# Row gathers one group ahead, unordered scatters and a ring of five weight buffers in the expert stage of a routed feed-forward kernel

## The chip, the cores and the metric

The kernel runs on one core of a Trainium2 chip. The metric is the device time of one execution in microseconds (us). Five engines of the core matter here: PE (TensorE, the matmuls; PEld is its weight load), DVE (VectorE), ACT (ScalarE), POOL (GpSimd, which issues the indirect transfers, that is gathers and scatters of rows by a list of row numbers) and SP (SyncE, which issues the plain transfers). Each engine works through its own instructions in order, and waits where an instruction needs what another engine or a transfer has not finished.

## What is computed

The reference runs three stages: an attention over packed tokens, a dense feed-forward with SiLU, and a routed one, in which every token goes to the one expert of eight that has its largest logit. Cut to what matters here:

```python
x = attention(q, k, v, p)                 # 4608 tokens x 512
x = silu(x @ w_in) @ w_out                # 512 -> 2048 -> 512
e_idx = argmax(x @ w_gate)                # one expert of 8 for each token
gate_w = softmax(x @ w_gate)[e_idx]
eom = sigmoid(x @ w_output_gate)
for e in range(8):                        # w1[e]: 512 x 1024, w2[e]: 1024 x 512
    mask = e_idx == e
    out[mask] = gate_w[mask] * eom[mask, e] * (relu(x[mask] @ w1[e]) @ w2[e])
```

Every matrix product is made of two or three products of high and low parts of its operands (names that end in `hi` and `lo`), so that float32 accuracy is kept.

## The kernel before

The first two stages run over eight batches of 576 tokens (`batch`, 16 steps `f` each). While they run, the finished rows go to an HBM table `xr` of one row per token (512 values and the routing weight). `place` works out for every token its place in its expert's list, and POOL scatters the token's number to that place in an HBM table of positions. Of that table there are two copies (`NPERM`), written in turn and added up when they are read.

The expert stage (`experts`, `groups`) works on groups of 576 tokens of one expert. Eight groups are always run (`NSTATIC`); more are run under a condition on the number of groups. The largest expert's first group, group 0, is started inside the last batch (`open_first`); the list of the other groups is known only when the last rows have been placed (`table`, `spread`).

One group has eight steps, one for each 128 of the 1024 hidden columns. `up(n)` is 24 matmuls into the accumulator `pu`, of which there is one, so that ACT and DVE must have read it (L992, L993) before the next `up`. `down(n)` is 14 matmuls into five accumulators `py` (blocks j of 128 tokens; block 4 has 64 tokens and is done first). The order on PE is written out by hand: `up(n+1)`, then `down(n)`. Between them lie numbered gaps: gap 2n+1 stands behind `up(n+1)`, gap 2n+2 behind `down(n)`. The dictionary `gaps` says what else is issued in each gap:

- `fetch(g)` gets a group's tokens: SP loads the 576 row numbers from the position tables (`fetch_ix`, L907 and L908) and the expert's output-gate row (`og`, L929), POOL adds the two copies (L910, L911) and gathers five blocks of rows from `xr` into `xg` (`fetch_x`, L920). There is one buffer `xg`. Fetch of group k+1 stands in gap 16k+1, which is one step into group k.
- `trx(g, j)` transposes block j on PE into one PSUM bank `px` (L960), ACT and DVE copy it out as high and low part into `xt` (two buffers, one for each of two groups), and DVE and ACT work out the output gate. For group k+1 the five blocks stand in gaps 16k+5 to 16k+13.
- `load_chunk` has SP load a quarter of an expert's weights, two transfers of 1 MB each (L945, L947), into a ring of seven buffers (`RING`). From step 5 on one is issued behind every odd `down`, into the buffer that this `down` has just finished with.

When the last `down` of a group ends, `put_out` scales the five blocks out of PSUM into `y` (ACT L1023 for j below 4; L1028 to L1030 for block 4), of which there are four buffers, and POOL scatters them to the rows of `out` (L1031). Every scatter writes the whole of `out` as far as the ordering of the program knows, so each waits until the one before it has landed.

Of the kernel before, what the change touches and what calls it, by code (L numbers as in the profile page):

```python
# [21 lines left out]
DM = 512  # L22
# [18 lines left out]
RING = 7  # L41
FG = F2 // 128
NPERM = 2
# [3 lines left out]
def constants():  # L47
# [14 lines left out]
    t -= NTOK // NPERM  # L62
# [27 lines left out]
class Kernel:  # L90
    def __init__(self, tc, ins, out):
        self.tc, self.nc, self.i, self.out = tc, tc.nc, ins, out
        nc = tc.nc
        self.ws1 = nc.dram_tensor("ws1", (E8, 4, 2, 128, F2), F32, kind="Internal").ap()
        self.ws2 = nc.dram_tensor("ws2", (E8, 4, 2, 128, 2 * DM), F32, kind="Internal").ap()
        self.perm = [nc.dram_tensor(f"perm{i}", (PROWS, PW), I32, kind="Internal").ap() for i in range(NPERM)]
        self.xr = nc.dram_tensor("xr", (NTOK + 1, XW), F32, kind="Internal").ap()
# [5 lines left out]
    def run(self):  # L103
# [18 lines left out]
        self.pick_i = cp.tile([128, 8], U32, name="pick_i")  # L122
        self.ptab = cp.tile([1, 2], I32, name="ptab")
# [52 lines left out]
    def setup_late(self):  # L176
# [6 lines left out]
        nc.gpsimd.memset(fill, NTOK // NPERM)  # L183
        for perm in self.perm:
            nc.sync.dma_start(perm.rearrange("(p c) w -> p (c w)", p=128).rearrange("p (h n) -> p h n", h=2),
                              fill.unsqueeze(1).to_broadcast([128, 2, n]))
# [18 lines left out]
    def open_first(self, f):  # L205
# [18 lines left out]
        if f > 12:  # L224
            for j in ((0, 1), (2, 3), (4,))[f - 13]:
                self.trx(0, j)

    def last_rows(self):
# [8 lines left out]
        acc = self.ps_acc.tile([128, 512], F32, tag="acc3", name="accL")  # L237
        side = {2: lambda: self.row_t(g, 3, 0), 4: lambda: self.row_logits(g, 3, 0), 5: lambda: self.row_logits2(g, (3, 0)),
# [547 lines left out]
    def place(self, g):  # L786
# [15 lines left out]
        def put():  # L802
# [48 lines left out]
    def experts(self):  # L851
# [19 lines left out]
    def more(self, lo, hi):  # L871
        self.nload = 4 * lo
        self.fetch(lo)
        for _ in range(RING):
            self.load_chunk()
        for j in range(GB):
            self.trx(lo, j)
        for k in range(lo, hi - 1):
            self.gaps[16 * k + 1] = [lambda k=k: self.fetch(k + 1)]
            for j in range(GB):  # L880
                self.gaps[16 * k + 5 + 2 * j] = [lambda k=k, j=j: self.trx(k + 1, j)]
        self.groups(lo, hi)
# [6 lines left out]
    def groups(self, lo, hi):  # L889
        self.up(FG * lo)  # L890
        self.gap(2 * FG * lo)
        for n in range(FG * lo, FG * hi):
# [4 lines left out]
            if n % 2 and n > 4 and self.nload < 4 * hi:  # L897
# [3 lines left out]
    def fetch_ix(self, g, off):  # L901
        nc = self.nc
        off = nc.values_load(off, engines=[ENG.SP], min_val=0, max_val=END)
        ix = self.rt.tile([128, NPERM, GB], I32, tag="xix_p", bufs=2, name="xix_p")
        at = self.rt.tile([128, GB], I32, tag="xix", bufs=3, name="xix")
        for i, perm in enumerate(self.perm):
            nc.sync.dma_start(ix[:, i, 0:4], perm[bass.ds(off, 512), 0:1].rearrange("(j p) w -> p (j w)", p=128))  # L907
            nc.sync.dma_start(ix[:64, i, 4:5], perm[bass.ds(off + 512, 64), 0:1])  # L908
# [41 lines left out]
    def trx(self, g, j):  # L950
        nc, rt = self.nc, self.rt
        x, og = self.x[g][0][j], self.x[g][1]
        if j == 0:
            self.sc[g] = rt.tile([128, GB, 4], F32, tag="sc", bufs=2, name="sc")
            if g == 1:
                t = self.p2.tile([128, 8 * GN], F32R, name="xt1")
                self.xt[1] = t.rearrange("p (h k t) -> p h k t", h=2, k=4)
        ps = self.bank("px")
        for k in range(4):
            nc.tensor.transpose(ps[:, 0, k * 128:k * 128 + 128], x[:, k * 128:k * 128 + 128], self.ident)  # L960
        n = min(128, GN - j * 128)
        src = ps[:, 0, :].rearrange("p (k t) -> p k t", k=4)[:, :, :n]
        hi, lo = [self.xt[g % 2][:, i, :, j * 128:j * 128 + n] for i in range(2)]
        nc.scalar.copy(out=hi, in_=src)
        nc.vector.tensor_tensor(out=lo, in0=src, in1=hi.bitcast(F32), op=ALU.subtract)
        junk = rt.tile([128, 512], BF16, tag="junk", bufs=1, name="junk")
# [3 lines left out]
        nc.scalar.activation(out=sc[:, 1:2], in_=sc[:, 0:1], func=AF.Exp, scale=-1.0)  # L970
        nc.vector.tensor_scalar(out=sc[:, 1:2], in0=sc[:, 1:2], scalar1=1.0, scalar2=None, op0=ALU.add)
        nc.vector.reciprocal(out=sc[:, 2:3], in_=sc[:, 1:2])
        nc.vector.tensor_tensor(out=sc[:, 3:4], in0=sc[:, 2:3], in1=x[:, DM:DM + 1], op=ALU.mult)
# [44 lines left out]
    def put_out(self, g, j):  # L1018
        nc, p2, acc = self.nc, self.p2, self.acc[j]
        at, s = self.at[g], self.sc[g][:, j, 3:4]  # L1020
        y = p2.tile([128, DM], F32, tag="y", bufs=4, name="y")
        if j < 4:
            nc.scalar.activation(out=y, in_=acc, func=AF.Copy, scale=s)  # L1023
# [45 lines left out]
```

## Time and profile before

| | us |
|---|---|
| median of 3 runs | 1380.42 (1375.12 to 1380.48) |
| the profiled execution, its own time | 1382.79 |
| its span, first to last instruction | 1381.0 |
| batches and last rows, before the first `up` | 828.48 |
| expert stage on PE, first `up` to last `down` | 529.6 (828.48 to 1358.09) |
| from there to the end of the span | 22.9 |

The profile describes one execution. Its own time is 1.8 us over its span; sums are made against that execution and then put against the median, which is 2.4 us lower. PE is busy for 90% of the span. [...]

### The profile page before, as it was taken

To read this page: it belongs to the slowest core of one execution; us is meant where nothing else is said; L and a number is where in the kernel's file an instruction comes from. 1 tells how busy PE (TensorE), PEld (TensorE's weight loads), DVE (VectorE), ACT (ScalarE), POOL (GpSimd) and SP (SyncE) were. 2 spreads that over 40 slices of the span, in tenths; PEclk is the share of its full clock that TensorE was granted. 3 is DMA by queue.
4 is the path that set the end of the run, shared out by engine and by line. 5 is a ranking of instruction groups with operands and counts; after the bars stand their busy time and mean duration, and the time that the engine had idled before them with its cause. 6 is when DMAs were issued, how large, how long until landed. Compare 5 with 4: busy or idle time off the path is not lost. (4 is left out here: it accounts for less than half of the span.)

```text
span 1381.0 us, 22060 instructions
## 1 busy us (share of the span) xinstructions
PE 1237.3 (90%) x8760; PEld 1022.5 (74%) x8760; DVE 661.6 (48%) x1495; ACT 477.3 (35%) x978; POOL 166.8 (12%) x191
## 2 busy tenths in 40 slices
PE   7788999999999999999999999769797979797993
PEld 3566777887877877777778878658696969696992
DVE  6888567457574667584584442313131313131310
ACT  3334645445544545454443331111111112121211
POOL 0225001001010001010003101120202020202011
PEclk9898999999999999999999999889898989898997
DMA  7565757467765658674655104974535353535011
GB/s 287 202 189 212 248 207 259 147 220 264 256 211 190 231 197 277 215 274 164 208 171 183 32 9 154 335 252 148 197 128 202 122 202 123 202 123 202 1 35 37
DMA packets 123863, 252.70 MB, mean 183 GB/s; under 512 B 18243, under 2 KB 69254, under 8 KB 123238
## 3 DMA queue, kind: packets, MB, share of 16 engines
q1 hardware_dynamic: 116454, 231.08, 48.7%
q0 software_dynamic: 7296, 20.11, 4.0%
q8 instruction: 71, 1.16, 0.4%
q14 instruction: 42, 0.34, 0.1%
HBM read 160.19 MB, written 91.10 MB: 182 GB/s over the span
## 5 line engine op out<-in xcount | busy, mean ns | idle before, releaser
L743 PE MATMUL acc<-wo,ghi 128*128 128x512 f32 x1024 | 318.7, 392 | 0.0
L987 PE MATMUL pu<-xt,w 128*128 128x256 f32 (+1 forms) x1536 | 225.7, 305 | 5.7 <-issue 4.0
L987 PEld LDWEIGHTS pu<-xt,w 128*128 128x128 f32 x1536 | 219.1, 198 | 13.5 <-issue 8.7
L743 PEld LDWEIGHTS acc<-wo,ghi 128*128 128x128 f32 x1024 | 193.6, 189 | 38.2
L993 DVE SCALAR_TENSOR_TENSOR xt<-pu,xt 128x512 fp32r<-128x512 f32 (+1 forms) x128 | 58.5, 457 | 327.9 <-ACT xt L992 302.7
L692 PE MATMUL ps_h<-a,m_hi 128*128 128x288 f32 x1024 | 214.4, 302 | 0.8 <-DVE a L658 0.8
L1012 PE MATMUL py<-w,xt 128*128 128x512 f32 x768 | 201.3, 412 | 14.2 <-ACT y L1023 9.5
L743 PE MATMUL acc<-wo,glo 128*128 128x512 f32 x512 | 212.3, 415 | 0.0
L1012 PEld LDWEIGHTS py<-w,xt 128*128 128x128 f32 x768 | 153.2, 200 | 53.8 <-ACT y L1023 16.8
L692 PE MATMUL ps_h<-a,m_lo 128*128 128x288 f32 x512 | 162.8, 318 | 22.1 <-DVE g L702 12.7
L692 PEld LDWEIGHTS ps_h<-a,m_hi 128*128 128x128 f32 x1024 | 170.2, 195 | 2.6 <-DVE a L658 1.0
L702 DVE SCALAR_TENSOR_TENSOR g<-g,ps_h 128x576 f32<-128x576 f32 x128 | 96.0, 750 | 129.0 <-ACT g L701 125.8
L992 ACT ACTIVATE xt<-pu 128x512 fp32r<-128x512 f32 (+1 forms) x128 | 52.5, 410 | 295.0 <-PE pu L987 242.2
L701 ACT ACTIVATE g<-ps_h 128x576 f32<-128x576 f32 x128 | 83.2, 650 | 168.5 <-PE ps_h L692 164.3
L692 PEld LDWEIGHTS ps_h<-a,m_lo 128*128 128x128 f32 x512 | 99.3, 194 | 48.2 <-DVE g L702 20.5
L743 PEld LDWEIGHTS acc<-wo,glo 128*128 128x128 f32 x512 | 96.7, 189 | 45.5 <-issue 27.7
L810 POOL DMA_INDIRECT perm<-tok,dsti x36 | 39.7, 1104 | 651.7 <-DVE dsti L807 478.7
L712 DVE TENSOR_TENSOR glo<-g,ghi 128x512 fp32r<-128x512 f32 x128 | 91.2, 713 | 38.1 <-ACT ghi L707 31.1
L707 ACT CAST ghi<-g 128x512 fp32r<-128x512 f32 x128 | 79.4, 620 | 73.3 <-DVE g L702 70.5
L1031 POOL DMA_INDIRECT out<-y,xix x40 | 39.2, 979 | 418.7 <-DVE y L1030 304.3
L512 DVE TENSOR_TENSOR mid<-mid,shi 128x1024 fp32r<-128x1024 f32 x48 | 58.8, 1225 | 43.3 <-ACT shi L511 43.3
L960 PE MATMUL px<-cst,xg 128*128 128x128 f32 x140 | 25.0, 308 | 47.0 <-DMA xg<-xr,xix 43.1
(188 smaller groups left out, 1197.7 us busy)
## 6 DMA issues: line engine op xcount, KB each, us to landing
w<-ws SPq DMA_DIRECT2D x64, 1024.0 KB
ws<-shi SPq DMA_DIRECT2D x64, 512.0 KB
mid<-in_w SPq DMA_DIRECT2D x48, 512.0 KB
ws<-mid SPq DMA_DIRECT2D x48, 512.0 KB
att_v<-in_v SPq DMA_DIRECT2D x15, 640.0 KB
att_k<-in_k SPq DMA_DIRECT2D x15, 576.0 KB
xr<-xr SPq DMA_DIRECT2D x32, 256.5 KB
stg<-in_w_in SPq DMA_DIRECT2D x16, 512.0 KB
```

The lines of the kernel that those rows point to most:

```text
L512: nc.vector.tensor_tensor(out=w.bitcast(F32R), in0=w, in1=hi.bitcast(F32), op=ALU.subtract)
L692: nc.tensor.matmul(ps[:, hf, :288], lw[:, qd, fs], rx[:, qd, ts], start=(i == 0), stop=(i == 5))
L701: nc.scalar.activation(out=g2, in_=ps[:, :, :288], func=AF.Tanh, scale=0.5)
L702: nc.vector.scalar_tensor_tensor(out=g2, in0=g2, scalar=1.0, in1=ps[:, :, :288], op0=ALU.add, op1=ALU.mult)
L707: self.nc.scalar.copy(out=hi, in_=self.graw[:, :512])
L712: self.nc.vector.tensor_tensor(out=lo, in0=self.graw[:, :512], in1=self.ghi.bitcast(F32), op=ALU.subtract)
L743: self.nc.tensor.matmul(acc, l, r, start=(first and i == 0), stop=(last and i == 2))
L810: nc.gpsimd.indirect_dma_start(out=self.perm[(i0 + r) % NPERM], out_offset=bass.IndirectOffsetOnAxis(ap=di[:, r:r + 1], axis=0), in_=self. ...
L987: nc.tensor.matmul(ps[:, hf, :m], w[:, k, r, fs], xt[:, l, k, ts], start=(i == 0), stop=(i == 11))
L992: nc.scalar.activation(out=hi, in_=src, func=AF.Relu)
L993: nc.vector.scalar_tensor_tensor(out=lo, in0=src, scalar=0.0, in1=hi.bitcast(F32), op0=ALU.max, op1=ALU.subtract)
L1012: nc.tensor.matmul(self.acc[j], hl[:, l + j * 128:l + j * 128 + 128], w[:, r], start=(first and i == 0), stop=(last and i == 2))
```

## The change

- `RING` is 5. Loads in group 0 stand in other gaps; from step 7 on they stand behind each odd `down` as before.
- `plan` fills the gaps. The transposes for group k+1 stay in gaps 16k+5 to 16k+13, except in group 0, where they stand in gaps 12, 13, 14, 14 and 14. The fetch that follows them is that of group k+2: it stands in gap 16k+15 (gap 16 in group 0), ahead of the last `down` and of the scatters of group k.
- Scatters to `out` and to the position table are declared independent of each other, and of the table there is one copy, whose row numbers are loaded straight into the list that the gathers read. A small POOL memset stands ahead of every scatter to the table.
- Block 4 is scaled and scattered from a buffer of its own (`yl`), so that the four `y` serve four blocks.
- `trx` takes several blocks that share a bank where there are two (last batch). The output gate's dot product is issued one gap later, and the rest of it one gap after that.
- `up(0)` is issued ahead of the last batch's left-over rows (`accL`).

```diff
-RING = 7
+RING = 5
...
-            for j in ((0, 1), (2, 3), (4,))[f - 13]:
-                self.trx(0, j)
+            self.trx(0, *((0, 1), (2, 3), (4,))[f - 13])
...
         acc = self.ps_acc.tile([128, 512], F32, tag="acc3", name="accL")
+        self.up(0)
...
-                nc.gpsimd.indirect_dma_start(
-                    out=self.perm[(i0 + r) % NPERM], out_offset=bass.IndirectOffsetOnAxis(ap=di[:, r:r + 1], axis=0),
+                nc.gpsimd.memset(self.spacer, 0)
+                put = nc.gpsimd.indirect_dma_start(
+                    out=self.perm, out_offset=bass.IndirectOffsetOnAxis(ap=di[:, r:r + 1], axis=0),
                     in_=self.tok[:, i0 + r:i0 + r + PW], in_offset=None)
+                self.rows_apart("perm", put.ins)
...
-        for i in (8, 9, 10, 11, 12):
+        for i in (10, 13, 14, 15):
             self.gaps[i] = [self.load_chunk]
-        for i, j in enumerate((0, 1, 2, 3, 4)):
-            self.gaps.setdefault(11 + (i + 1) // 2, []).append(lambda j=j: self.trx(1, j))
-        for k in range(1, NSTATIC - 1):
-            self.gaps[16 * k + 1] = [lambda k=k: self.fetch(k + 1)]
-            for j in range(GB):
-                self.gaps[16 * k + 5 + 2 * j] = [lambda k=k, j=j: self.trx(k + 1, j)]
+        self.plan(0, NSTATIC, 12, 1)
...
+    def plan(self, lo, hi, first=5, every=2):
+        for k in range(lo, hi - 1):
+            at = [16 * k + (first + j * every if k == lo else 5 + 2 * j) for j in range(GB)]
+            for j, n in enumerate(at):
+                n = min(n, 16 * k + 14)
+                self.gaps.setdefault(n, []).append(lambda k=k, j=j: self.trx(k + 1, j))
+            if k + 2 < hi:
+                self.gaps.setdefault(min(at[-1], 16 * k + 14) + 2, []).append(lambda k=k: self.fetch(k + 2))
+
+    def rows_apart(self, name, put):
+        self.tc.declare_no_dep(put, group=name, reason="every token has a row of its own")
+        self.tc.add_to_no_dep_group(name, put)
...
-        ix = self.rt.tile([128, NPERM, GB], I32, tag="xix_p", bufs=2, name="xix_p")
...
-        nc.gpsimd.tensor_tensor(out=at[:, 0:4], in0=ix[:, 0, 0:4], in1=ix[:, 1, 0:4], op=ALU.add)
-        nc.gpsimd.tensor_tensor(out=at[:64, 4:5], in0=ix[:64, 0, 4:5], in1=ix[:64, 1, 4:5], op=ALU.add)
+        nc.sync.dma_start(at[:, 0:4], self.perm[bass.ds(off, 512), 0:1].rearrange("(j p) w -> p (j w)", p=128))
+        nc.sync.dma_start(at[:64, 4:5], self.perm[bass.ds(off + 512, 64), 0:1])
...
+            self.late.append(lambda j=j: self.gate_dot(g, j, xs[j], og))
...
-            nc.vector.tensor_scalar(out=y[:n], in0=t[:n], scalar1=s[:n], scalar2=None, op0=ALU.mult)
-        nc.gpsimd.indirect_dma_start(out=self.out, out_offset=bass.IndirectOffsetOnAxis(ap=at[:n, j:j + 1], axis=0),
-                                     in_=y[:n], in_offset=None, bounds_check=NTOK - 1, oob_is_err=False)
+            nc.vector.tensor_scalar(out=y[:n], in0=y[:n], scalar1=s[:n], scalar2=None, op0=ALU.mult)
+        put = nc.gpsimd.indirect_dma_start(out=self.out, out_offset=bass.IndirectOffsetOnAxis(ap=at[:n, j:j + 1], axis=0),
+                                           in_=y[:n], in_offset=None, bounds_check=NTOK - 1, oob_is_err=False)
+        self.rows_apart("out", put.ins)
```

On POOL, around the end of a middle group, the kernel before has the group's five scatters (the last two of one group stand here), then the adding up of the row numbers (`xix`) and the five gathers for the next group, whose transposes are due in the same group:

```order
L1031 DMA out<-y_9557,xix_8753 4608x512
L1031 DMA out<-y_9565,xix_8753 4608x512
L909 MEMSET xix_9613 64x1
L910 TENSOR_TENSOR xix_9613<-xix_p_9612 128x4
L911 TENSOR_TENSOR xix_9613<-xix_p_9612 64x1
L920 DMA xg_9623<-xr,xix_9613 128x513 x5
L1031 DMA out<-y_10022,xix_9121 4608x512
```

In the changed kernel the gathers stand ahead of the group's scatters, and what they bring is transposed a group later; the first scatter comes from `yl`:

```order
L1046 DMA out<-y_9598,xix_8781 4608x512
L914 MEMSET xix_10036 64x1
L925 DMA xg_10042<-xr,xix_10036 128x513 x5
L1046 DMA out<-yl_10050,xix_9108 4608x512
L1046 DMA out<-y_10060,xix_9108 4608x512
L1046 DMA out<-y_10068,xix_9108 4608x512
```

The two additions are gone, and gathers and scatters have changed places.

On SP, at the same place, the kernel before loads the weights behind the group's last `down` (`w_9570`), then the row numbers from both copies, then `og`:

```order
L945 DMA w_9570<-ws1 128x8x256
L947 ISA
L947 DMA w_9570<-ws2 128x2x1024
L903 TENSOR_LOAD tab_89
L903 ISA x2
L907 ISA
L907 DMA xix_p_9612<-perm0 128x4x1
```

In the changed kernel the row numbers and `og` stand between the load behind step 5 of the group (`w_9922`) and the one behind its last step (`w_10089`):

```order
L952 DMA w_9922<-ws2 128x2x1024
L941 TENSOR_LOAD tab_90
L941 ISA x2
...
L915 DMA xix_10036<-perm 128x4x1
L916 ISA
L916 DMA xix_10036<-perm 64x1
L934 ISA
L934 DMA og_10040<-in_wog 128x512
L950 ISA
L950 DMA w_10089<-ws1 128x8x256
```

The row numbers have moved ahead by one weight load, that is by two steps, and are two transfers where there were four.

## Rows read from the trace of the kernel before

**Rows 1.** Waits of PE, 872 us to the end: total us, times, longest.

```profile
PE px L960 <- DMA xg<-xr,xix: 43.1, 7, 9.8
PE py L1012 <- ACT y L1023: 9.5, 4, 2.9
PE py L1012 <- DMA w<-ws: 4.7, 2, 2.4
PE pu L987 <- issue: 4.0, 5, 0.8
```

**Rows 2.** POOL's timeline, 1030 to 1080 us: start, length, instruction, [idle before].

```profile
1039.51 0.93 POOL L1031 DMA_INDIRECT out<-y,xix  x1 [39.69 <-DVE y L1030]
1047.28 1.01 POOL L1031 DMA_INDIRECT out<-y,xix  x1 [6.85 <-ACT y L1023]
...
1060.56 1.00 POOL L920 DMA_INDIRECT xg<-xr,xix  x1 [1.23 <-issue]
1061.86 0.96 POOL L920 DMA_INDIRECT xg<-xr,xix  x1 [0.30 <-issue]
```

**Rows 3.** ACT's timeline at the same boundary.

```profile
1046.58 0.69 ACT L1023 ACTIVATE y<-py,sc 128x512 f32<-128x512 f32 x1 [6.71 <-DMA out<-y,xix]
```

**Rows 4.** PE's timeline: first transposes of groups 2, 4 and 7, and what follows.

```profile
931.77 1.11 PE L960 MATMUL px<-cst,xg 128*128 128x128 f32 x4 [9.79 <-DMA xg<-xr,xix]
...
1067.24 1.12 PE L960 MATMUL px<-cst,xg 128*128 128x128 f32 x4 [6.24 <-DMA xg<-xr,xix]
...
1269.43 1.12 PE L960 MATMUL px<-cst,xg 128*128 128x128 f32 x4 [6.33 <-DMA xg<-xr,xix]
...
1275.95 3.34 PE L987 MATMUL pu<-xt,w 128*128 128x256 f32 x24
1279.13 0.60 PE L960 MATMUL px<-cst,xg 128*128 128x128 f32 x4
```

**Rows 5.** Stretches: us, busy PE, PEld, DVE, ACT, POOL, granted clock, DMA share, GB/s.

```profile
875.00:931.80 56.80, 40.51 (x211) 35.20 (x211) 14.28 (x42) 10.64 (x25) 8.15 (x11) 0.83 0.86 302
999.50:1067.20 67.70, 58.50 (x324) 51.91 (x324) 17.09 (x48) 12.87 (x31) 10.43 (x14) 0.90 0.47 165
1282.84:1289.71 6.87, 6.87 (x43) 6.24 (x42) 2.69 (x8) 1.49 (x5) 0.00 (x0) 1.00 0.00 1
1316.18:1322.55 6.37, 6.37 (x40) 5.80 (x38) 0.92 (x2) 0.82 (x2) 1.97 (x2) 1.00 0.13 47
1341.77:1348.22 6.45, 6.45 (x39) 5.81 (x38) 0.92 (x2) 0.82 (x2) 0.00 (x0) 1.00 0.01 3
828.48:931.77 103.29, 81.06 (x466) 72.11 (x464) 25.61 (x91) 17.66 (x42) 17.65 (x24) 0.90 0.73 247
```

**Rows 6.** ACT's timeline where the last left-over rows leave PSUM.

```profile
828.68 0.60 ACT L754 ACTIVATE xr<-accL 128x512 f32<-128x512 f32 x1 [2.65 <-PE accL L743]
```

**Rows 7.** PE's timeline: second of two transposes in one gap, last batch and group 0.

```profile
795.33 0.66 PE L960 MATMUL px<-cst,xs 128*128 128x128 f32 x4 [1.40 <-DVE xt L965]
...
882.84 0.66 PE L960 MATMUL px<-cst,xg 128*128 128x128 f32 x4 [1.40 <-DVE xt L965]
```

**Rows 8.** SP's timeline: first weight load behind fetch(1), and a fetch in group 2.

```profile
864.78 0.37 SPq L945 DMA_DIRECT2D w<-ws  x1
...
972.13 0.37 SPq L945 DMA_DIRECT2D w<-ws  x1
...
973.99 0.37 SPq L907 DMA_DIRECT2D xix_p<-perm  x1
```

**Rows 9.** The scatters to `out` (L1031): time from issue to landing.

```profile
DMA to landing us min/median/max: 2.7/3.5/4.9
```

**Rows 10.** POOL's timeline, the last group's scatters: first and last of five.

```profile
1357.42 0.91 POOL L1031 DMA_INDIRECT out<-y,xix  x1 [31.43 <-DVE y L1030]
...
1373.04 0.98 POOL L1031 DMA_INDIRECT out<-y,xix  x1 [2.53 <-DMA out<-y,xix]
```

**Rows 11.** SP's waits, 872 us to the end: total us, times, longest.

```profile
SPq L945 <- PE py L1012: 299.4, 22, 24.6
```

More of the change, by code (lines that the diff above doesn't have):

```diff
@@ L40 @@
 NSTATIC = 8
-RING = 7
+RING = 5
 FG = F2 // 128
-NPERM = 2
 PW = 16
@@ L95, in __init__ @@
         self.ws2 = nc.dram_tensor("ws2", (E8, 4, 2, 128, 2 * DM), F32, kind="Internal").ap()
-        self.perm = [nc.dram_tensor(f"perm{i}", (PROWS, PW), I32, kind="Internal").ap() for i in range(NPERM)]
+        self.perm = nc.dram_tensor("perm", (PROWS, PW), I32, kind="Internal").ap()
         self.xr = nc.dram_tensor("xr", (NTOK + 1, XW), F32, kind="Internal").ap()
@@ L122, in run @@
         self.pick_i = cp.tile([128, 8], U32, name="pick_i")
+        self.spacer = cp.tile([128, 1], I32, name="spacer")
         self.ptab = cp.tile([1, 2], I32, name="ptab")
@@ L873, in more @@
         self.fetch(lo)
-        for _ in range(RING):
+        for _ in range(4):
             self.load_chunk()
@@ L877, in more @@
             self.trx(lo, j)
-        for k in range(lo, hi - 1):
[L879 to L882, printed above, removed]
+        run(self.late)
+        run(self.late)
+        if lo + 1 < hi:
+            self.fetch(lo + 1)
+        self.plan(lo, hi)
+        self.up(FG * lo)
+        self.groups(lo, hi)
+    def plan(self, lo, hi, first=5, every=2):
+        for k in range(lo, hi - 1):
+            at = [16 * k + (first + j * every if k == lo else 5 + 2 * j) for j in range(GB)]
[7 more added lines that the diff above has]
+        self.tc.add_to_no_dep_group(name, put)
     def gap(self, n):
@@ L896, in groups @@
             self.down(n)
-            if n % 2 and n > 4 and self.nload < 4 * hi:
+            if n % 2 and n > 6 and self.nload < 4 * hi:
                 self.load_chunk()
@@ L957, in trx, with gate_dot @@
                 self.xt[1] = t.rearrange("p (h k t) -> p h k t", h=2, k=4)
+        xs, og = self.x[g]
         ps = self.bank("px")
[L959 to L966, printed above, removed]
+        for i, j in enumerate(js):
+            for k in range(4):
+                nc.tensor.transpose(ps[:, i, k * 128:k * 128 + 128], xs[j][:, k * 128:k * 128 + 128], self.ident)
+        for i, j in enumerate(js):
+            n = min(128, GN - j * 128)
+            src = ps[:, i, :].rearrange("p (k t) -> p k t", k=4)[:, :, :n]
+            hi, lo = [self.xt[g % 2][:, h, :, j * 128:j * 128 + n] for h in range(2)]
+            nc.scalar.copy(out=hi, in_=src)
+            nc.vector.tensor_tensor(out=lo, in0=src, in1=hi.bitcast(F32), op=ALU.subtract)
+            self.late.append(lambda j=j: self.gate_dot(g, j, xs[j], og))
+    def gate_dot(self, g, j, x, og):
+        nc = self.nc
+        junk = self.rt.tile([128, 512], BF16, tag="junk", bufs=1, name="junk")
         sc = self.sc[g][:, j, :]
@@ L969, in trx, with gate @@
                                        op0=ALU.mult, op1=ALU.add, accum_out=sc[:, 0:1])
[L970 to L973, printed above, removed]
+        def gate():
+            nc.scalar.activation(out=sc[:, 1:2], in_=sc[:, 0:1], func=AF.Exp, scale=-1.0)
+            nc.vector.tensor_scalar(out=sc[:, 1:2], in0=sc[:, 1:2], scalar1=1.0, scalar2=None, op0=ALU.add)
+            nc.vector.reciprocal(out=sc[:, 2:3], in_=sc[:, 1:2])
+            nc.vector.tensor_tensor(out=sc[:, 3:4], in0=sc[:, 2:3], in1=x[:, DM:DM + 1], op=ALU.mult)
+        self.late.append(gate)
     def up(self, n):
@@ L1020, in put_out @@
         at, s = self.at[g], self.sc[g][:, j, 3:4]
-        y = p2.tile([128, DM], F32, tag="y", bufs=4, name="y")
         if j < 4:
+            y = p2.tile([128, DM], F32, tag="y", bufs=4, name="y")
             nc.scalar.activation(out=y, in_=acc, func=AF.Copy, scale=s)
```

23 lines of the change are left out of this document (8 added, 15 removed).

## The prediction

> **What bounds the kernel now.** I read the waits of PE first, since PE is the engine that is nearly always busy, and only from 872 us on, where groups follow each other [rows 1]. Three things stand out: PE waits for gathered rows 7 times (43.1 us), for the scaling of the last block 6 times (9.5 and 4.7 us; two of the six are put down to a weight transfer, but stand at the same place of a group), and a little around those. POOL's timeline says why both happen [rows 2]: the first scatter of a group goes out at 1039.51, the second only at 1047.28, and the five gathers of the next group stand behind the fifth scatter and begin at 1060.56. ACT's row between them is the reason of the second wait: five blocks share four `y`, so the scaling of the last block waited 6.71 us for the first scatter to land [rows 3], and PE needs that accumulator again in the next group's first `down`. So POOL's chain of scatters is what holds back the gathers, and the gathers hold back PE once in each group.
>
> What an undisturbed group costs is read from stretches in which nothing waits [rows 5]: a step without a transpose 6.37 and 6.45, taken as 6.42, and one with a transpose 6.87. A group has three of the first and five of the second: 3 x 6.42 + 5 x 6.87 = 53.6 us. What it costs now is read from two rows [rows 4]: the first transpose of group 2 starts at 931.77 and that of group 7 at 1269.43, five groups in 337.66, or 67.5 each. The 13.9 us between are the two waits and the clock: the granted clock over such a group is 0.90, over an undisturbed step 1.00 [rows 5]. How much the clock takes can be read once: from the first transpose of group 7 to the next `pu` it is 6.52 us, and one step on, with the clock back, 3.71 (1279.13 to 1282.84) [rows 4, 5]. A wait of some 6 us is thus followed by 2.8 us of slow matmuls.
>
> **The change part by part.** The sum goes from the profiled execution, 1382.79.
>
> *Gathers one group ahead, five middle groups.* The gathers of group k+2 stand in gap 16k+15 and are needed six half steps later, 6 x 3.2 = 19 us. What they have to wait for is: the last read of the single `xg` by the gate (one gap after the dot; a few short operations of DVE and ACT behind that `up`, taken as 2.5 us), the row numbers, and themselves. The row numbers are issued 1.9 us behind the weight load of step 5 (972.13 to 973.99 [rows 8]), which is three half steps, 10 us, before the gap. Behind a load of 2 MB at 302 GB/s [rows 5], an estimate of 7 us, they land about when the gap comes. From the issue of the first gather to the transpose that waited for it was 6.7 us (1060.56 [rows 2] to 1067.24 [rows 4]); the others follow 1.3 us apart [rows 2] and are needed 6.9 us apart. So 2.5 + 6.7 = 9.2 against 19: 10 us of room. *Scatters and `yl`:* the four `y` of a group were scattered a group earlier, so ACT waits for none; the five scatters now stand behind five gathers, 10 x 1.3 = 13 us of POOL per group, and nobody waits for them before the next group's end. Both waits go and with them the clock. What is late next is PE itself. 337.66 - 5 x 53.6 = **-69.6**.
>
> *The first stretch*, first `up` to the first transposes of group 2, is 103.29 us [rows 5]. It holds 12 `up` and 10 `down` (10 x 6.42 + 2 x 3.2 = 70.6), five blocks of transposes (5 x 0.45 = 2.3) and 1.4 of small matmuls: 74.3. What I leave in it: the left-over rows are transposed straight behind `accL` now that `up(0)` has moved, so ACT's 0.60 copy [rows 6] and its two handovers are bare, 1.0 (in exchange `up(1)` no longer waits for `up(0)` to be read); three blocks of transposes stand in gap 14 on one bank, so two wait 1.40 each [rows 7], 2.8; and group 2's gather. That one alone has no room: it is fetched in gap 16, behind the weight load that waits for the last `down`, and five half steps (16 us) before it is needed. Five chunks, issued from 864.78 on [rows 8], and the gathers are 11.7 MB, at 302 GB/s [rows 5] 39 us, so the row numbers land at about 904 and the first tokens 6.7 us later at 910.5, against 828.5 + 78.1 = 906.6. I take 5 us and 2.8 of clock; bounds are nothing, if the ring of five makes less of a queue, and the 9.79 that stands there now [rows 4] with its clock, 12.6. Group 1's rows are due 2.4 us later than now, need no addition and waited 4.4 us there: nothing left. 74.3 + 1.0 + 2.8 + 7.8 = 85.9, so **-17.4** (-25 to -13).
>
> *After group 7's transposes begin* nothing waits today either; the slow matmuls of 6.52 become 3.71: **-2.8**.
>
> *The end.* The last group's scatters start at 1357.42 and, the fifth, at 1373.04 [rows 10]. Without waiting for each other they follow 1.3 us apart like the gathers [rows 2], the fifth at 1362.6; its data is there by 1359. What follows the fifth stays. **-10.4** (-8 to -11). Each scatter lands 3.5 us after its issue [rows 9], and that is the pace of the chain now. [...]
>
> *Last batch.* Two pairs of transposes now lie in one bank of two halves; the second of a pair waited 1.40 us [rows 7] and does not any more: **-2.8** (0 to -4). The later gates take DVE and ACT off the path there; no PE wait hangs on them.
>
> *Edits taken at nothing.* One position table saves 2.4 MB of filling in the first batch, two row-number loads for each group and 36 waits of POOL's scatters in batches where no engine waits for POOL; the memsets ahead of them are 0.1 us of an idle engine. *Ring of five:* a buffer is freed by one `down` and refilled for an `up` seven steps on, 7 x 6.42 = 45 us, against 7 us for the load itself. SP spends 299.4 us waiting for PE to free a buffer [rows 11], so it is early everywhere. The rate has to rise: a group moves 165 GB/s x 67.7 us = 11.2 MB [rows 5], in 53.6 us that is 208 GB/s at a DMA share of 0.47 x 67.7 / 53.6 = 0.59; a stretch with 302 GB/s at 0.86 exists [rows 5]. Cover gone, each us costs a us.
>
> Sum: -69.6 - 17.4 - 2.8 - 10.4 - 2.8 = -103.0, so 1279.8 for an execution like the profiled one. The median of the runs lies 2.4 lower: **1277**.
>
> **The rivals.**
> *A, gathers still late in every group.* If the queue of weights ahead of the row numbers, or the gate's last read of `xg`, eats the 10 us of room, the wait comes back under another name. For it: row numbers and loads share the transfer engines. Against: the load ahead of them is 10 us older. If half of the 6 us wait and its clock return six times: 6 x (3 + 1.8) = 29, 1306.
> *B, transfers become the pace.* If groups cannot move more than the 165 GB/s they move now [rows 5], a group stays at 67.7 us, and only the start, the end and the batch are won: 1380 - 33 = 1347. Against: 302 GB/s [rows 5].
> *C, slower.* SP is in order, and the fetch now stands ahead of the load behind the last `down`. If its list of row numbers, one of three, or `og` came free only after a landing that itself is late, SP would hold that load. It decides from 38 us on (45 of lead less 7 of load); each us more is a PE wait in six groups. To lose the whole 103 takes 17 us more, SP held for 55 us, a whole group; at 60 us it is 6 x (22 + 2.8) = 149, 1426. Against it: SP's rows show waits for PE and next to nothing else [rows 11], and the list that fetch k+2 overwrites was last used by the scatters of group k-1, a whole group earlier.
> *D, scatters still in a row.* The fourth and fifth still wait for a semaphore, one of eight in turn. If that is as slow as the chain is now, the end keeps its 10.4, and the middle groups lose nothing, since POOL has 53.6 us for ten transfers: 1288.
>
> **How the numbers follow.** Forecast 0.80, A 0.10, D 0.04, B 0.04, C 0.02. Forecast's own bounds: group 2's gather -8 to +5, the last batch and end +-3, the level of the runs +-3, so 1264 to 1290; to leave out no more than 2 in 10 with D and part of A the range goes to 1302. Faster by over 0.5% (about what a measurement of this kernel can tell from no change): all but C and a little of A and B beyond their price, 0.97; same 0.01; slower 0.02.
>
> **What would show it.** In the profile of the changed kernel: groups of 53 to 54 us on PE with the granted clock at 1.00, no wait of PE for `xg` from group 3 on and one of 0 to 10 us for group 2; gathers ahead of scatters on POOL, all 1.3 us apart; no wait of ACT for `out`; the end some 12.5 us behind the last `down` instead of 22.9; PE's waits for `w` at nothing. A wait of PE for `xg` in every group makes it A, waits for `w` or a DMA share near 0.9 make it B, and SP's wait for anything but PE makes it C.

## The result, and the profile after

The changed kernel takes **1308.08 us** (median of 4 runs, 1306.18 to 1310.35) where the kernel before takes 1377.77 (a fourth run has joined the three of the table above); the ratio is 0.9495, 95% interval 0.9464 to 0.9525. That is 31 us more than forecast and outside the range. The profiled execution took 1306.18, its span is 1304.4. Between the profiled executions the gain is 76.6 us, 26.4 short of the 103.0 forecast; the rest of the 31 is the level of the runs, since the forecast put the median 2.4 under the profiled execution and it lies 1.9 above.

PE's waits from 872 us on, the view of [rows 1] (total us, times, longest), are these now:

```profile
PE pu L1002 <- DVE xt L1008: 17.3, 5, 3.6
PE px L966 <- DVE xt L972: 2.8, 2, 1.4
PE py L1027 <- issue: 0.2, 1, 0.2
```

The 43.1 us for gathered rows are gone, and so are the waits for `y`. In their place stands one that the kernel before did not have: once at each of five group ends, 3.5 us, before an `up`, for DVE to have read the one accumulator `pu`. POOL's timeline at the first of these ends (start, length, instruction, [idle before]), the place of [rows 2]:

```profile
947.49 0.94 POOL L925 DMA_INDIRECT xg<-xr,xix  x1 [37.09 <-DVE yl L1044]
...
952.49 0.94 POOL L925 DMA_INDIRECT xg<-xr,xix  x1 [0.30 <-issue]
953.74 0.93 POOL L1046 DMA_INDIRECT out<-yl,xix  x1 [0.30 <-issue]
...
958.89 0.98 POOL L1046 DMA_INDIRECT out<-y,xix  x1 [0.30 <-issue]
```

Ten indirect transfers in one row, 1.25 to 1.3 us apart, as forecast. PE's timeline beside it:

```profile
947.46 3.33 PE L1002 MATMUL pu<-xt,w 128*128 128x256 f32 x24
...
953.88 3.33 PE L1002 MATMUL pu<-xt,w 128*128 128x256 f32 x24
957.05 0.62 PE L1024 MATMUL py<-w,xt 128*128 128x512 f32 x2
...
964.05 6.03 PE L1002 MATMUL pu<-xt,w 128*128 128x256 f32 x24 [3.13 <-DVE xt L1008]
```

and ACT's:

```profile
950.88 0.60 ACT L1007 ACTIVATE xt<-pu 128x512 fp32r<-128x512 f32 x1 [1.70 <-PE pu L1002]
962.07 0.60 ACT L1007 ACTIVATE xt<-pu 128x512 fp32r<-128x512 f32 x1 [9.61 <-PE py L1027]
```

The `up` that starts at 953.88 ends at 957.21. ACT, which has nothing else to do, reads it at 962.07, 4.9 us later; one `up` earlier it was 0.1 us (947.46 + 3.33 = 950.79, read at 950.88). So neither DVE, which the wait names, nor ACT was the cause: PE's own signal that `pu` is done came late. (A signal is here an update of a semaphore that another engine's instruction waits for; the trace holds records of them with their times.) The records of PE's semaphore say the same: the signals due at 957.21 and at the end of the next `down` are set at 961.99 and 962.13. The `up` behind the wait then takes 6.03 us for 3.33, at the lower clock (granted clock 0.52 over it, 1.00 over the one before). A middle group is 58.90 us at a granted clock of 0.97 (stretch from the first transposes of group 3 to those of group 4; columns as in [rows 5]):

```profile
969.93:1028.83 58.90, 55.43 (x325) 50.17 (x324) 16.31 (x48) 12.20 (x31) 9.78 (x11) 0.97 0.54 189
```

At the end of the span, where [rows 10] had 15.6 us from the first scatter to the fifth, there are 5.1:

```profile
1291.85 0.91 POOL L1046 DMA_INDIRECT out<-yl,xix  x1 [41.00 <-DVE yl L1045]
...
1296.94 0.98 POOL L1046 DMA_INDIRECT out<-y,xix  x1 [0.30 <-issue]
```

The gain by the terms of the prediction, each from one profiled execution; the last column is the same kernel on another chip (S), which the experiments lead to:

| us | predicted | here | other chip |
|---|---|---|---|
| five middle groups (337.66 before) | -69.6 | -41.0 (296.65) | -69.3 (268.32) |
| first stretch, from the first left-over row, or `up(0)` where that is now ahead of it (118.87 before) | -17.4 | -23.9 | -23.8 |
| first transposes of group 7 to the last scatters (87.99 before) | -2.8 | -2.6 | -2.6 |
| end | -10.4 | -11.0 | -11.0 |
| all that is ahead of the left-over rows (812.90 before) | -2.8 | +2.0 | -6.4 |
| sum | -103.0 | -76.6 | -113.2 |

### The profile page after: what moved, and what is told of

It reads as the page before. It is cut to its first block, busy times and chain, and to the rows that moved or that the text cites. A ratio compares the mean times of both kernels' runs of the same rounds, so it can differ in the third digit from the quotient of the medians.

```text
span 1304.4 us, 22047 instructions
## 1 busy us (share of the span) xinstructions
PE 1213.3 (93%) x8758; PEld 1003.9 (77%) x8760; DVE 656.5 (50%) x1495; ACT 472.6 (36%) x978; POOL 167.7 (13%) x211
## 5 line engine op out<-in xcount | busy, mean ns | idle before, releaser
L690 PE MATMUL ps_h<-a,m_hi 128*128 128x288 f32 x1024 | 211.2, 299 | 0.8 <-DVE a L656 0.8
L1027 PE MATMUL py<-w,xt 128*128 128x512 f32 x768 | 188.2, 393 | 0.2 <-issue 0.2
L1027 PEld LDWEIGHTS py<-w,xt 128*128 128x128 f32 x768 | 144.2, 188 | 34.3 <-issue 0.6
L690 PEld LDWEIGHTS ps_h<-a,m_hi 128*128 128x128 f32 x1024 | 167.3, 192 | 2.5 <-DVE a L656 1.0
L710 DVE TENSOR_TENSOR glo<-g,ghi 128x512 fp32r<-128x512 f32 x128 | 91.5, 715 | 38.2 <-ACT ghi L705 33.7
L925 POOL DMA_INDIRECT xg<-xr,xix x35 | 33.4, 955 | 239.6 <-DVE yl L1044 214.7
L561 PE MATMUL ps_m<-w_in,ppt 64*32 64x256 f32 x1008 | 44.8, 402 | 10.3 <-ACT e L577 6.1
```

What stands on the lines that cost most here:

```text
L561: self.nc.tensor.matmul(ps[32 * c:32 * c + 32, r, :n], lhs(rows, c), rhs(rows, c), start=True, stop=True)
L690: nc.tensor.matmul(ps[:, hf, :288], lw[:, qd, fs], rx[:, qd, ts], start=(i == 0), stop=(i == 5))
L710: self.nc.vector.tensor_tensor(out=lo, in0=self.graw[:, :512], in1=self.ghi.bitcast(F32), op=ALU.subtract)
L1027: nc.tensor.matmul(self.acc[j], hl[:, l + j * 128:l + j * 128 + 128], w[:, r], start=(first and i == 0), stop=(last and i == 2))
```

## Experiments

Seven chips were used, here called P to V. Each ratio is to the kernel before on the same chip; whether the result above came from one of the seven is not known, so a comparison with its 1308.08 is one across chips. **Theory N**: a long unbroken row of indirect transfers on POOL holds back PE's signals until it is over. **Rivals**: T, it is the traffic of ten such transfers beside a weight load; later U (their number within some longer time), V (the chip matters too) and R (the records of semaphores are the cause, a conjecture). A chip that holds signals is, below, one whose trace shows PE's signals late behind such rows.

| kernel | chip | us (median) | ratio to before, 95% |
|---|---|---|---|
| pause between gathers and scatters (e1_pause) | P | 1278.82 | 0.9272 to 0.9328 |
| fetch behind the scatters (e2_fetch_behind) | P | 1310.85 | 0.9474 to 0.9545 |
| gathers spread (e3_spread) | P | 1278.14 | 0.9260 to 0.9312 |
| pause in the table's scatters (e4_table_pause) | P | 1301.57 | 0.9435 to 0.9479 |
| pauses of five lengths (e5_pause_length) | R | 1271.43 | |
| pause at five places (e6_pause_place) | R | 1269.99 | |
| scatters to `out` in order (e7_out_in_order) | R | 1296.98 | 0.9386 to 0.9439 |
| spread, and pause in the table (e8_spread_and_table) | R | 1270.51 | 0.9199 to 0.9255 |
| the changed kernel (r1_changed_again) | S | 1272.13 | 0.9207 to 0.9272 |
| as e5 and e6 (r2_pause_length, r3_pause_place) | S | 1270.45, 1270.20 | |
| as e8 (r4_spread_and_table) | S | 1271.38 | 0.9204 to 0.9274 |
| rows and bursts (e9_a) | Q | 1290.13 | |
| the changed kernel (r5_changed) | T | 1271.07 | 0.9208 to 0.9258 |
| as e8 (r6_spread_and_table) | T | 1271.32 | 0.9212 to 0.9257 |
| short pauses (e10_short_pauses) | T | 1268.99 | 0.9197 to 0.9244 |
| as e10 (r7_short_pauses, r8_short_pauses) | U, V | 1268.41, 1268.32 | 0.9191 to 0.9228, 0.9177 to 0.9231 |

**A pause between the two rows.** At the ends of groups 1 to 5, in `put_out`, with a `pause` of 128 x 512:

```diff
...
+        if j == 4 and 1 <= g < 6:
+            for _ in range(7):
+                nc.gpsimd.memset(self.pause, 0)
         put = nc.gpsimd.indirect_dma_start(out=self.out, out_offset=bass.IndirectOffsetOnAxis(ap=at[:n, j:j + 1], axis=0),
```

> The changed kernel, with seven POOL memsets (about 3.8 us) between the five gathers and the five scatters at the end of groups 1 to 5. In the changed kernel each of these five boundaries costs 5.7 us: PE's signal that an `up` is done comes 4.8 us late. Theory N (POOL's unbroken row of more than five indirect transfers holds PE's signals back from about the fifth on until 1 to 2 us behind the last): two rows of five with a pause hold back little that anybody waits for, no PE wait for DVE xt at the group ends, 1308 - 5 x 5.7 = 1280. Rival T (it is the traffic of ten row transfers beside a weight load, however they are spaced): 1308, the wait of 3.5 us stays.

1278.82 us, and the five middle groups take 268.5 us. POOL and ACT at the same group end:

```profile
953.27 4.04 POOL L1049 MEMSET pause<- 128x512 int32 x7
957.57 0.93 POOL L1050 DMA_INDIRECT out<-yl,xix  x1 [0.26 <-issue]
```

```profile
957.08 0.60 ACT L1008 ACTIVATE xt<-pu 128x512 fp32r<-128x512 f32 x1 [4.85 <-PE pu L1003]
```

The same ten transfers and the same loads stand around it; only POOL does something else for 4 us between the rows, and ACT's read of `pu` at 957.08 follows the `up` (ending 956.99) by 0.1. No wait of an `up` for DVE is left among PE's waits. That chip P holds signals where the row is whole is shown by e4 below, which leaves the ten unbroken; PE's waits there:

```profile
PE pu L1003 <- DVE xt L1009: 17.7, 5, 3.7
```

On one chip, then, the five waits stand with the whole row and go with the pause. T falls.

**The fetch one step later**, behind the scatters:

```diff
-                self.gaps.setdefault(min(at[-1], 16 * k + 14) + 2, []).append(lambda k=k: self.fetch(k + 2))
+                self.gaps.setdefault(16 * k + (16 if k == lo else 17), []).append(lambda k=k: self.fetch(k + 2))
```

> The changed kernel with the fetch of group k+2 one step later, in gap 16k+17, behind the scatters of group k and not ahead of them, as it stands at the boundary of groups 0 and 1, where PE waits for nothing. Theory N: rows of five and five with POOL waiting for row numbers between them, 1280; if the row numbers come late behind the weight load, PE waits for xg instead, up to 5 us in each of five groups, 1305. Rival T: 1308 with the wait for DVE xt as before.

At the group ends no `up` waited for DVE, where the result had five waits of 3.5 us, and the time was lost again another way. PE's waits:

```profile
PE px L966 <- DMA xg<-xr,xix: 23.3, 6, 5.0
PE px L966 <- DVE xt L972: 2.8, 2, 1.4
```

POOL waited 5.72 us for the row numbers, which now stand behind a weight load, and the gathers began at 965.80, 18 us later than those of e1 (947.26). That fetch and gathers stand one step earlier is thus worth 32 us (1310.85 to 1278.82), and rows of five and five with a wait of 5.72 us between them held nothing that PE needed.

**Gathers one at a time**, the row numbers (`fetch_rows`) ahead of them:

```diff
...
+                self.gaps.setdefault(16 * k + 3, []).append(lambda k=k: self.fetch_rows(k + 2))
+                for j in range(4):
+                    self.gaps.setdefault(16 * k + 7 + 2 * j, []).append(lambda k=k, j=j: self.fetch_block(k + 2, j))
+                self.gaps.setdefault(16 * k + 15, []).append(lambda k=k: self.fetch_og(k + 2))
+                self.gaps.setdefault(16 * k + 19, []).append(lambda k=k: self.fetch_block(k + 2, 4))
...
```

> The changed kernel with the gathers of groups 3 to 7 spread: row numbers loaded in gap 16k+3, one gather in each of the gaps 16k+7, 9, 11 and 13, behind the last read of the block it overwrites, the fifth behind the scatters in gap 16k+19. The scatters stay five in a row. Theory N: no row longer than five, no wait at the group ends, 1280 or a little under. Rival T (scatters beside the weight load are enough): 3.5 us of wait and 2.2 us of clock at each group end stay, 1308.

1278.14, as N said: the five scatters are still in a row (with the fifth gather behind them it is six) and the load still beside them. It is the weaker test, since at the group end looked at (949.16 to 956.63) no signal of PE falls due in the second half of that row.

**The position table's scatters.** The batches lost 4.8 us against the forecast. With a `spacer` of 128 x 128 and fourteen memsets, 3.63 us, ahead of the fourth scatter:

```diff
...
-                nc.gpsimd.memset(self.spacer, 0)
+                for _ in range(14 if r == 3 else 1):
+                    nc.gpsimd.memset(self.spacer if r == 3 else self.spacer[:, :1], 0)
```

> The changed kernel with fourteen small POOL memsets (2 to 3 us) ahead of the fourth scatter to the position table in each batch. In the changed kernel PE waits 1.4 to 1.6 us at 343.6, 541.1 and 736.3 us, each 2.8 us behind the fifth of five such scatters, and not in the batches with four. Theory N: rows of three and two hold nothing back, the three waits go, 1308 - 4.6 = 1303. Rival T (the scatters being unordered is enough): the waits move or stay, 1308.

ACT's read of `ps_h` around 340 us, behind a row of five, in the changed kernel (first) and in this one (second):

```profile
342.12 0.65 ACT L699 ACTIVATE g<-ps_h 128x576 f32<-128x576 f32 x1 [1.70 <-PE acc L741]
```

```profile
340.24 0.66 ACT L699 ACTIVATE g<-ps_h 128x576 f32<-128x576 f32 x1
```

The same read of PSUM goes 1.9 us earlier, since PE's signal is there. 1301.57 is 6.5 us under the result, but on another chip. On chip P itself the three batches whose table takes five scatters last 90.4, 90.3 and 91.4 us with the pause and 92.0, 91.9 and 93.4 in e1, where the table is as changed (first `glo` matmul of `acc` in one batch to that in the next): 5.2 us in all, where 4.6 were expected. The one small memset that the change has ahead of each of these scatters does not break a row: in it the next transfer still follows after 0.3 us.

**Length and place of the pause, and scatters in order.** These ran on chip R, with a combined version. The first, with as many memsets as the group's number:

```diff
...
+        if j == 4 and 1 <= g < 6:
+            for _ in range(g):
+                nc.gpsimd.memset(self.pause, 0)
```

> The changed kernel with a pause between gathers and scatters that is one POOL memset (0.6 us) long at the end of group 1, two at group 2, up to five (2.9 us) at group 5. Theory N (a row holds PE's signals until 1.1 us behind its last transfer, and a pause longer than that begins a new row): the PE wait of 3.5 us stays at group 1, perhaps at group 2, and is gone at groups 3 to 5; some 1308 - 3.5 x 5.7 = 1288. Rival U (the hold hangs on how many transfers have been issued within some longer time): it shrinks a little from group to group and is still there at group 5, about 1300.

The second has the seven memsets of e1 at another place in each group:

> The changed kernel with the same seven memsets (4.1 us) at another place of the ten transfers in each group end: behind 2, 3, 4, 6 and 8 of them at the ends of groups 1 to 5. PE's signals are due about 3.3, 9.7 and 16 us behind the start of the first gather. Theory N with the fourth or fifth in a row as the beginning: 2 then 8, the signal at 16 us meets the seventh or eighth of the second row and is held; 3 then 7 and 4 then 6 likewise, by 1 to 2 us; 6 then 4 and 8 then 2 end their long row before or about when the signal at 9.7 us is due, so nothing or up to 2 us. Rival U (any ten within this time): all five group ends are alike.

The third leaves out one line, and the fourth takes the edits of e3 and e4 together:

```diff
-        self.rows_apart("out", put.ins)
```

> The changed kernel with the scatters to `out` ordered again: each waits until the one before has landed, 3.5 us apart as before. All else is as changed, the gathers ahead of them and `yl` too. Theory N: with the scatters apart nothing is held back in the middle groups, 53.6 us each, and only the end loses its 10.4 again: 1308 - 5 x 5.7 + 10.4 = 1290; so in the middle groups the scatters' independence is what costs. Rival T (gathers and scatters beside the weight load): the waits stay and the end is lost, 1318.

> Two of the edits together: gathers of groups 3 to 7 one at a time in gaps 16k+7 to 16k+19 (alone 1278.1), and a pause of some 3.8 us ahead of the fourth scatter to the position table (alone 1301.6, 6.5 under the changed kernel). By theory N they act at different places and add up: 1308 - 30 - 6.5 = 1271.6. If they are one effect counted twice, 1278.

The first two told nothing of a pause, and much of the chip: 1271.43 and 1269.99, and not one signal of PE late, neither where the row was broken by a short pause alone nor behind the five table scatters that both kernels leave as the change has them. So N does not hold everywhere. With the scatters in order the middle groups take 270.8 us, 2.5 more than without late signals (268.3); the kernel loses 10.6 at the end, and 14.8 at group 2, which I had not expected:

```profile
PE px L966 <- DMA xg<-xr,xix: 14.8, 1, 14.8
```

Group 2's gathers are the only ones behind scatters (gap 16), and wait for all five. The independence of the scatters is worth those two places, about 25 us; in the middle groups it is worth 2.5, and the row that it makes possible cost 28 on the result's chip (e7 did not run on a chip that holds signals). The combined version took 1270.51.

**The changed kernel again.**

> The changed kernel itself, unedited, beside the next three on one chip. In the second group of experiments no row of transfers held anything back, not even rows that held PE's signals in the first group (five scatters to the position table, which two of those kernels leave as the change has them). Theory V (the hold hangs on the chip or its state as well as on the row): where rows of five show on-time signals, the changed kernel takes about 1276 with no PE wait for DVE xt; where they are held, 1308 again. Theory N (the row alone decides): 1308 with five waits of 3.5 us, here as before.

1272.13 us on chip S. PE's only wait from 872 us on, and the boundary at which 4.9 us were lost, ACT's reads of `pu`:

```profile
PE px L966 <- DVE xt L972: 2.8, 2, 1.4
```

```profile
942.58 0.60 ACT L1007 ACTIVATE xt<-pu 128x512 fp32r<-128x512 f32 x1 [1.70 <-PE pu L1002]
949.01 0.60 ACT L1007 ACTIVATE xt<-pu 128x512 fp32r<-128x512 f32 x1 [4.85 <-PE pu L1002]
955.44 0.60 ACT L1007 ACTIVATE xt<-pu 128x512 fp32r<-128x512 f32 x1 [4.85 <-PE pu L1002]
```

One every 6.43 us, right behind each `up`, while POOL issues the same ten transfers in one row from 939.19 to 951.58. A group is 53.71 us at full clock:

```profile
955.18:1008.89 53.71, 53.71 (x327) 48.76 (x324) 16.30 (x48) 12.22 (x31) 9.80 (x11) 1.00 0.59 209
```

V holds. The other kernels on this chip, the two with pauses (1270.45 and 1270.20) and the combined one (1271.38), lay with it, as their expectations had it for a chip that holds nothing:

> The version with spread gathers and a pause in the table's scatters, once more (1270.5). It has no row longer than five anywhere, and none of five where PE's signal is awaited, so by both theories it is the same on any chip: 1271.

The two kinds of chip can be told apart in the trace itself. The profile's row for the weight loads, first of the result above, then of the same kernel on chip S:

```profile
w<-ws SPq DMA_DIRECT2D x64, 1024.0 KB
```

```profile
w<-ws SPq DMA_DIRECT2D x64, 1024.0 KB, 7.4
```

The first has no time of landing, because records of semaphores are missing. The 116 indirect transfers set their semaphores 16 times each, 1856 records. The result's trace has 932 of them, those of chip P 996 to 1637, that of chip Q 1187; those of chips R to V have 1849 to 1856. Of SP's plain transfers the result's trace has 6162 records of 6624, that of S 6612. The kernel before has 1787 of the 1856 and 6425 of SP's 6896.

**Rows and bursts**, on chip Q. The rows are cut by memsets as in e1, at other places, and in group 7 SP issues bursts:

```diff
...
+    def burst(self, i):
+        nc = self.nc
+        t = self.p2.tile([128, 10, 4], I32, tag=f"burst{i}", name="burst")
+        nc.vector.memset(t, 0)
+        for m in range((5, 10)[i]):
+            nc.sync.dma_start(t[:, m], self.perm[m * 512:m * 512 + 512, 0:1].rearrange("(j p) w -> p (j w)", p=128))
...
```

> The changed kernel with a different row of ten transfers at each group end: group 1 unbroken, group 2 with 0.6 us of POOL memset between gathers and scatters, group 3 with 1.2 us, group 4 with 4.1 us behind the fourth transfer, group 5 with 4.1 us behind the sixth; and in group 7, where POOL is idle, SP issues 5 and then 10 small transfers (512 packets of 4 bytes each) in a row. On a chip that holds signals, by theory N (row on POOL): a wait of 3.5 us at group 1 and 2, less or none at 3, a signal 1 to 2 us late at group 4, none at 5, and nothing at the bursts; 1285 to 1300. By theory R (records of the transfers' semaphores, which were missing in the traces of the chip with held signals and complete on the other two, choke the path that PE's signals take): the bursts hold PE's signals as well. On a chip that does not hold signals: about 1272, every signal on time, and all records of the transfers there.

Chip Q holds signals. The pauses of groups 2 and 3 in POOL's timeline:

```profile
1011.96 0.95 POOL L931 DMA_INDIRECT xg<-xr,xix  x1 [0.30 <-issue]
1012.95 0.53 POOL L1061 MEMSET pause<- 128x512 int32 x1
1013.64 0.94 POOL L1062 DMA_INDIRECT out<-yl,xix  x1 [0.16 <-issue]
...
1072.31 0.95 POOL L931 DMA_INDIRECT xg<-xr,xix  x1 [0.30 <-issue]
1073.30 1.12 POOL L1061 MEMSET pause<- 128x512 int32 x2
1074.68 0.93 POOL L1062 DMA_INDIRECT out<-yl,xix  x1 [0.25 <-issue]
```

and ACT's reads of `pu` at groups 1 to 4:

```profile
962.42 0.60 ACT L1020 ACTIVATE xt<-pu 128x512 fp32r<-128x512 f32 x1 [9.56 <-PE py L1040]
...
1021.48 0.60 ACT L1020 ACTIVATE xt<-pu 128x512 fp32r<-128x512 f32 x1 [9.69 <-remote]
...
1076.92 0.60 ACT L1020 ACTIVATE xt<-pu 128x512 fp32r<-128x512 f32 x1 [4.79 <-PE pu L1015]
...
1138.53 0.60 ACT L1020 ACTIVATE xt<-pu 128x512 fp32r<-128x512 f32 x1 [6.33 <-PE px L979]
```

The `up`s ended at 957.61, 1016.59, 1076.82 and 1136.92. Unbroken: 4.8 us late. With 0.73 us between the rows (1012.91 to 1013.64): 4.9 late. With 1.42 us (1073.26 to 1074.68): on time, so U falls, as far as one group end can show it. Four then six: the signal fell due during the last transfer of the six and came 1.6 late, and PE had enough in hand not to wait. Six then four: on time for `pu`. The bursts held nothing, and their 240 semaphore records are complete; five transfers were issued within 2.1 us and ten within 5.7, closer together than POOL's rows, and PE's signals due at 1241.21 and 1263.76, in the middle of them, were set 0.01 us later. So many small transfers alone did not do it, which speaks against R as it was put:

```profile
1239.94 25.66 SPq L950 DMA_DIRECT2D burst<-perm  x15
```

**The versions that remain.** Beside the changed kernel a third time, the combined one and the smallest edit, eight memsets of 128 x 128 (2.1 us) ahead of block 4's scatter and ahead of the fourth scatter to the table:

> The changed kernel, unedited, a third time. Theory N on a chip that holds signals: 1308, five PE waits of 3.5 us at the group ends and some hundreds of the transfers' semaphore records missing. On a chip that holds none: 1272, no such wait, records complete.

> Spread gathers and a 3.6 us pause in the table's scatters, once more (1270.5 and 1271.4 on chips that hold nothing). No row is longer than six and none lies where PE's signal is due, so 1271 on a chip that holds signals too; if the hold needs no row, 1285 or more there.

> The smallest edit: the changed kernel with eight small POOL memsets (2.1 us) ahead of the first scatter to `out` of each group and ahead of the fourth scatter to the position table. The pause of 1.4 us between the ends and starts of the two rows was enough in the look before, 0.7 was not. Theory N: on a chip that holds signals 1308 - 28 - 6.5 = 1273; on another 1272, since the pauses lie on an idle engine and cost nothing.

Chip T holds nothing: 1271.07, 1271.32 and 1268.99. The last also ran on two more chips:

> The version with 2.1 us pauses at two places, once more (1269.0 on a chip that holds no signals). The profile's count of semaphore records tells which kind of chip it is. Theory N: 1273 on a chip that holds signals (the changed kernel 1308 there), 1269 on another. If a row of five is already too long where PE's signal is due, some 1 to 2 us per group end come back: 1280.

> The same kernel as the run before, on whatever chip comes. Theory N: 1273 on a chip that holds signals and 1268 on one that does not; with late signals at every group end in spite of the pauses, 1280 or more on a holding chip.

Neither holds signals: 1268.41 and 1268.32. So the short pauses cost nothing; that they also take the loss away on a holding chip is shown only by their parts, e1, e4 and the pause of 1.42 us in e9, not by this kernel.

## Why the prediction missed, point by point

- **Five middle groups, -69.6, measured -41.0: the step that failed.** "Nobody waits for them before the next group's end" and "What is late next is PE itself" were said of five scatters behind five gathers. Nobody waited for a scatter, but everybody waited for PE's signal behind them: 5.7 us in each group (59.3 for 53.7), 3.5 of wait and the rest clock, 28.3 in all. Without the hold the term is right to 0.5 us: 268.5 with the pause on chip P, 268.3 for the unedited kernel on chip S, 268 forecast. The room of 10 us for the gathers was there, and no wait for `xg` came back.
- **The last batch and "edits taken at nothing".** I gave the table's scatters no price, since "no engine waits for POOL" there. Three batches have five of them in a row, and from the first `glo` matmul of one batch to that of the next these take 92.0, 91.9 and 93.4 us in the result, 90.4, 90.2 and 91.5 in the kernel before, and 90.3, 90.3 and 91.4 on chip S: 5.2 us lost to the same cause. The last batch's own term was right: from the first transposes to the left-over rows it is 19.57 us before (793.33 to 812.90), 16.37 in the result (798.52 to 814.89) and 16.37 on S (790.18 to 806.55), -3.2 for -2.8. The other 3.2 that S gained lie in the batches ahead, two of which differ by 1.5 and 2.0 us among runs whose kernels are alike up to there, so it is not clear of noise.
- **The first stretch, -17.4, measured -23.9.** I had charged 7.8 for a late gather of group 2. It was not late, even where signals are held: no wait for `xg` stands among the result's waits of PE. The bound that had nothing for that gather, -25, was the nearer one. e7 shows what would make it late: scatters in order.
- **End and group 7's start**: -10.4 and -2.8, measured -11.0 and -2.6. The scatters' pace is their issue, 1.3 us, as [rows 2] had it for gathers.
- **Rivals.** A gave 1306, close to the result by luck, for a reason that did not occur. B did not occur: 209 GB/s per group on chip S. Of C its sign is there, and small. SP waits for DVE too, ahead of `og`, on S as in the result:

```profile
SPq L934 <- DVE sc L979: 12.5, 5, 2.6
```

The longest is 2.6 us where C's price begins at 38, and PE waits for no weights. D, tried as e7, gave 1297 and not 1288; its price at group 2 was missing.

So the sum describes the kernel on a chip that holds nothing (1272.1 on S, 1271.1 on T, inside the range), and missed the recorded result by one mechanism. A sign of the chip's kind may have stood on the page of the kernel before: no landing time for the weight loads (no trace of that kernel from another chip is there to compare). And one late signal can be read in its trace, in the last batch. ACT's read of `ps_m`, in the kernel before, in the result and on chip S:

```profile
786.83 0.59 ACT L670 CAST m_hi<-ps_m 128x512 fp32r<-128x512 f32 x1 [0.46 <-PE ps_m L563]
```

```profile
792.06 0.59 ACT L668 CAST m_hi<-ps_m 128x512 fp32r<-128x512 f32 x1 [0.50 <-PE ps_m L561]
```

```profile
783.17 0.59 ACT L668 CAST m_hi<-ps_m 128x512 fp32r<-128x512 f32 x1
```

The matmuls ended at 786.21, 791.40 and 783.06: 0.6 and 0.7 us late on the first two, 0.1 on S. But the kernel before takes 1376.6 to 1378.1 us on every chip, and a row that shows 0.6 us once could not price 5.7 in each group.

## What to carry to other kernels

When a change lets POOL issue indirect transfers closer together, look behind each row for the signals that other engines wait for; a releaser that had long been done, with nothing between, may be a late signal (here one of 4.8 us). Two microseconds of other work on POOL between rows of five were free on chips without late signals (1268.99 us with them on T, 1271.07 without); where signals were late, 1.42 us (Q) and 4.04 (P) took the loss away, and 0.73 (Q) did not. Compare more than one chip before a gain or a loss of some per cent is put down to the code.

## What the runs showed of the hardware

- On some chips PE's semaphore signals came late while POOL issued indirect transfers 1.25 to 1.3 us apart. In each row of ten of the result the signal due in the eighth was set 4.7 to 4.8 us late, 1.9 to 2.1 us behind the row; behind rows of five late signals were set up to 1.2 us after the row. What had piled up was then set 0.05 us apart (five signals from 342.03 to 342.24) or 0.14 (961.99 and 962.13). Seen for the result, on P and on Q, and not on R, S, T, U and V; whether it is the chip or a state of it at the time isn't told apart.
- Theory N is too narrow: it did not take a long row. A signal due 0.2 us into the third of the table's five scatters (337.60 in the result; the scatter starts at 337.39) was 1.3 us late for DVE, where on chip S it was 0.1 (336.64); in e4, with a row of three, the same signal was set at 338.83 for 337.59. The late read of `ps_m` above falls into the first scatter of a row, beside plain transfers of SP. DVE's reads of `ps_s`, in the result and on S:

```profile
338.93 0.76 DVE L576 TENSOR_REDUCE sm<-ps_s 128x2 f32<-128x576 f32 x1 [1.76 <-PE ps_s L561]
```

```profile
336.75 0.76 DVE L576 TENSOR_REDUCE sm<-ps_s 128x2 f32<-128x576 f32 x1 [0.61 <-PE ps_s L561]
```

- Not every signal within a row was late: among scatters to `out` one due 0.04 us into the fifth was on time (e1, 1017.13 and 1017.09). Nor was it every engine: while PE's signals due from 339.39 on were held to 342.03, DVE's due at 339.69 was set at 339.70.
- Five gathers alone did it (the first fetch of the result: row over at 871.63, signal due at 872.27, set at 872.83), five scatters to `out` (e1: 963.71, 963.41, 964.77), and four small ones to the table (the result: 838.49, 838.91, 839.47); fifteen plain transfers from SP did not.
- The cause is open. Where the changed kernel or an edit of it had late signals, the trace had lost records of the indirect transfers' semaphores, 12 to 50% of them, and 6 to 7% of those of SP's; where nearly all were there (1849 or more of 1856), none was late. Whether the recording itself has a part in it is not shown, since no run here shows the kernel without its recording.
